# Splitting the float64 weights of a linear-attention and convolution kernel in seven wide tiles instead of fourteen

## The chip, the cores and the metric

The kernel runs on one core of a Trainium2 chip. The time is device microseconds (us) of one execution; a profile of one further execution gives the trace. Line numbers such as L296 are lines of the kernel before the change; the changed kernel has the same statements some 4 to 13 lines further down.

## What is computed

Two stages follow each other. The first is a gated linear attention for 4 batches, 8 heads, 768 time steps and a head size of 48; the second takes its output as x, multiplies by a weight, filters along time, gates and multiplies by a second weight.

```
f = 1 / (1 + exp(-f_logit))
for t in range(768):
    state = f[t][:, None] * state + outer(k[t], v[t])       # 48 x 48 per head
    y[t] = q[t] @ state
x = y with the heads side by side                            # 4 x 768 x 384
h = max(x @ w_in, 0)                                         # 4 x 768 x 1024
conv[t] = conv_w[0]*h[t-1] + conv_w[1]*h[t] + conv_w[2]*h[t+1]
out = (h / (1 + exp(-conv))) @ w_out                         # 4 x 768 x 384
```

`w_in` (384x1024), `conv_w` (3x1024) and `w_out` (1024x384) arrive as float64, two 32-bit words per element.

## The kernel before

**Attention.** Time is cut in 24 chunks of 128 steps (n = 0 to 23, six per batch). For each chunk ScalarE takes two functions of the gate tile `fb` (L376, L378), VectorE scans it (L394), ScalarE makes two exponentials `e` (L397, L399), GpSimd copies their last column to `ft_all` (L401), and VectorE scales keys and queries with them (`kq`, L403). TensorE transposes the keys into `ss` (L409) and forms the scores `A` (L420); VectorE keeps the causal half as `am` (L423). TensorE then sums carried state (L435) and values (L442) into `Y` and makes the new state (L464). ScalarE and VectorE write `Y` as a high and a low part into `xT` (L452, L454), and VectorE updates the state `st` (L471, L474, L476). `Y` and `A` are single PSUM buffers.

**Second stage.** It goes by half batches u = 0 to 7 of three chunks each. When the three chunks of u are in `xT`, six DMAs gather the rows of a fourth slot (L484). For each of 8 blocks f of 128 columns, nine matmuls (L514) form x @ w_in in one of two PSUM buffers `mm`; ScalarE copies it out with a relu into `hb` (L524) and multiplies (L530), VectorE adds two more taps (L534), and for each pair of blocks ScalarE takes a tanh (L538) and VectorE multiplies (L540). A 128-row tile of the output takes a high and a low copy of the gates (L557, L561), 24 matmuls with w_out (L570), a copy to `ob` (L576) and a DMA. All eight blocks of w_out are needed from its first tile on.

**Weights.** Each float64 tile is turned into a float32 sum of two parts, high and low, that TensorE takes in `wi` and `wo`. `split_f64` does it: the raw words come by DMA (`load_raw`, L329); the absolute value of the upper words (ScalarE, L290), a clamp (VectorE, L292), an exclusive or with a shift (L294), a second absolute value (ScalarE, L296), sign and exponent put together (L297), the exponent alone (L299), the high part (ScalarE, L306), and the lower word scaled by the exponent (`ob`, L313). In mode 'd' three matmuls (L318 to L320) then add the pieces in `mm`, and ScalarE or VectorE copies the low part out (L324); in mode 'v' VectorE does it alone (L308, L310, L311). w_in is 6 tiles of 512 columns, w_out 8 tiles of 384; eleven tiles take mode 'd', the last three mode 'v'. The raw words and all intermediate tiles live in buffers that the second stage uses later (`xT`, `g`, `gx`, `ob`).

**Order.** `Plan` decides the order of the instructions on all engines before the program is built: each step has a key from the table `CFG` (a time in chunks plus an offset), an estimated duration in ns, and the buffers that it takes from rings; `Plan.order` plays this through and writes the instructions in the order that it finds. Each engine then works its list strictly in order, and so does SyncE (SP), which issues all DMAs.

Of the kernel before, what the change touches and what calls it, by code (L numbers as in the profile page):

```python
# [174 lines left out]
def gla_moe_kernel(ctx, tc, kq_in, v_in, f_in, w_in, conv_w, w_out, out):  # L175
# [99 lines left out]
    def split_f64(raw, at, r, n, key, need, hi, lo, nm, mode=None):  # L275
        ids = ("raw", raw), ("ms", nm), ("low", nm), ("mm", "pz" + nm)
# [15 lines left out]
        o = step("DVE", 170 + 250 * x, lambda e: V.tensor_scalar(  # L292
            ms(0).bitcast(F32), ms(0).bitcast(F32), F64_LO, F64_HI, ALU.max, ALU.min), [o], use=(1,))
        o = step("DVE", 130 + 385 * x, lambda e: V.tensor_scalar(  # L294
            ms(0), ms(0), 1 << 27, 3, ALU.bitwise_xor, ALU.logical_shift_left), [o], use=(1,))
        o = step("ACT", 160 + 470 * x, lambda e: A.activation(ms(0).bitcast(F32), ms(0).bitcast(F32), AF.Abs), [o], use=(1,))  # L296
        m = step("DVE", 150 + 530 * x, lambda e: V.scalar_tensor_tensor(  # L297
            ms(0), pr(1), -(1 << 31), ms(0), ALU.bitwise_and, ALU.bitwise_or), [o])
        s = step("DVE", 160 + 250 * x, lambda e: V.tensor_scalar(ms(1), ms(0), -(1 << 23), None, ALU.bitwise_and), [m],  # L299
                 use=(1,))  # L300
        mf, sf = (lambda: ms(0).bitcast(F32)), (lambda: ms(1).bitcast(F32))
        if lo is None:
            o = step("DVE", 150 + 530 * x, lambda e: V.scalar_tensor_tensor(
                sf(), pr(0).bitcast(U32), 2.0 ** -52, sf(), ALU.mult, ALU.mult), [s])
            return step("DVE", 150 + 530 * x, lambda e: V.tensor_tensor(hi(), mf(), sf(), ALU.add), [o], use=(1,))
        h = step("ACT", 160 + 460 * x, lambda e: A.copy(hi(), mf()), [m], use=(1,))  # L306
        if mode == "v":
            o = step("DVE", 150 + 530 * x, lambda e: V.scalar_tensor_tensor(  # L308
                sf(), pr(0).bitcast(U32), 2.0 ** -52, sf(), ALU.mult, ALU.mult), [s])
            d = step("DVE", 150 + 530 * x, lambda e: V.tensor_tensor(mf(), mf(), hi().bitcast(F32), ALU.subtract), [h], use=(1,))  # L310
            return step("DVE", 150 + 530 * x, lambda e: V.tensor_tensor(lo(), mf(), sf(), ALU.add), [o, d], use=(1,))  # L311
        low = lambda: plan.buf(ids[2])[:, :n]
        o = step("DVE", 150 + 530 * x, lambda e: V.scalar_tensor_tensor(  # L313
            low(), pr(0).bitcast(U32), 2.0 ** -52, sf(), ALU.mult, ALU.mult), [s], take=(2,))
        pz = lambda: plan.buf(ids[3])[:, :n]

        def join(e):
            nc.tensor.matmul(pz(), ident, mf(), start=True, stop=False)  # L318
            nc.tensor.matmul(pz(), negr, hi(), start=False, stop=False)
            nc.tensor.matmul(pz(), idr, low(), start=False, stop=True)  # L320
# [11 lines left out]
    W_IN, W_OUT = [[None] * KT for _ in range(DFF // WC)], [None] * NF  # L332
    for i in range(DFF // WC):
        for kt in range(KT):
            cs = slice(i * WC, (i + 1) * WC)
            o = load_raw(("wi", i), kt * RW, w_in[kt * P:(kt + 1) * P, cs].bitcast(I32), P, (0.01 * kt, "w1", i), 512, kt == 0)
            W_IN[i][kt] = split_f64(("wi", i), kt * RW, P, WC, (0, "w1s", KT * i + kt), o, lambda kt=kt, cs=cs: wi[:, kt, 0, cs],
                                    lambda kt=kt, cs=cs: wi[:, kt, 1, cs], f"wi{kt}_{i}", CFG["ez"][KT * i + kt])
# [408 lines left out]
```

## Time and profile before

| what | value |
|---|---|
| three timed runs | 339.94 us median (338.13 to 341.12) |
| the profiled execution | 338.65 us, its span 336.9 us, granted TensorE clock 0.994 |
| TensorE matmul (PE) busy | 309.9 us, 92% of the span, 2703 instructions |
| VectorE (DVE) busy | 273.2 us, 81%, 417 instructions |
| ScalarE (ACT) busy | 234.0 us, 69%, 395 instructions |
| GpSimd (POOL) busy | 39.3 us, 12%, 69 instructions |
| chain that ended last | PE 58%, ACT 17%, DMA 13%, DVE 8% |

The span is the time from the first to the last instruction of the profiled execution; 1.75 us of its time lie outside. A busy PE is not yet a PE at its peak: its matmuls are pipelined and a wait shows mainly as the distance between starts. In rows of the time line the first number is the start and the second the duration, both in us; in rows of windows each engine has its busy time and its instruction count.

### The profile page before, as it was taken

Reading aid. Unit: us, or ns where it says so; the run is one execution under the profiler, and the core shown is the slowest. Engines: PE = TensorE matmul, PEld = TensorE weight load, DVE = VectorE, ACT = ScalarE, POOL = GpSimd, SP = SyncE. Lnnn points to the kernel's source line nnn. Section 1 sums busy time; section 2 is a strip of 40 time slices with the busy share of each in tenths; the row PEclk is TensorE's granted clock in tenths of the full one; section 3 lists DMA queues with packets and bytes.
Section 4 is the critical chain, followed back from the end, with each engine's and each line's share of the span. In section 5 each row is a group of like instructions: output and inputs, shape, how many; then the busy total and the mean of one; then the engine's idle time right before and its main releaser. Section 6 shows DMA issues by size and latency. Waiting matters only on the chain.

```text
span 336.9 us, 6805 instructions
## 1 busy us (share of the span) xinstructions
PE 309.9 (92%) x2703; PEld 284.6 (84%) x2703; DVE 273.2 (81%) x417; ACT 234.0 (69%) x395; POOL 39.3 (12%) x69
## 2 busy tenths in 40 slices
PE   0498799989999999999999999999999999999992
PEld 0365478788899899889889999999899999999992
DVE  7989999989999999999999958288768179695210
ACT  6979897689979975799966755464575386684320
POOL 2400100000630006503010210000000001000000
PEclk9999999999999999999999999999999999999997
DMA  7999744620063121655242521121100002101111
GB/s 231 405 402 392 285 136 143 201 106 25 6 211 111 42 70 47 201 161 167 89 137 72 175 60 47 47 74 40 37 0 2 23 26 58 47 2 48 47 46 36
DMA packets 17452, 37.51 MB, mean 111 GB/s; under 512 B 2540, under 2 KB 8708, under 8 KB 17412
## 3 DMA queue, kind: packets, MB, share of 16 engines
q1 hardware_dynamic: 17412, 37.00, 32.6%
q8 instruction: 23, 0.38, 0.5%
q14 instruction: 17, 0.14, 0.1%
HBM read 29.91 MB, written 4.72 MB: 103 GB/s over the span
## 4 chain that ended last, share of the span: by engine, by line
PE 58%; ACT 17%; DMA 13%; DVE 8%; issue 2%; SPq 1%; ACTq 0%; DVEq 0%
PE mm L570 28%; PE mm L514 19%; DMA g<-in_moe_w_out_dram 5%; PE Y L442 4%; ACT g L530 3%; PE A L420 3%; DMA fb<-in_f_logit_dram 3%; DMA xT<-in_moe_w_in_dram 2%; DMA v<-in_v_dram 2%; PE Y L435 2%; ACT hb L524 2%; ACT g L538 1%; DVE am L423 1%; DVE kq L403 1%; ACT fb L376 1%
## 5 line engine op out<-in xcount | busy, mean ns | idle before, releaser
L514 PE MATMUL mm<-xT,wi 128*128 128x384 f32 x576 | 108.1, 341 | 2.3 <-ACT hb L524 1.8
L514 PEld LDWEIGHTS mm<-xT,wi 128*128 128x128 f32 x576 | 99.6, 188 | 4.7 <-ACT hb L524 3.0
L570 PE MATMUL mm<-wo,gx 128*128 128x384 f32 x576 | 103.5, 339 | 0.0
L570 PEld LDWEIGHTS mm<-wo,gx 128*128 128x128 f32 x576 | 101.6, 188 | 0.2 <-issue 0.2
L534 DVE SCALAR_TENSOR_TENSOR g<-hb,cw,g 128x385 f32<-128x385 f32 (+1 forms) x128 | 74.4, 614 | 13.1 <-ACT g L530 11.7
L561 DVE TENSOR_TENSOR gx<-g,gx 128x1024 fp32r<-128x1024 f32 (+2 forms) x28 | 29.8, 1071 | 26.4 <-PE mm L570 23.9
L524 ACT ACTIVATE hb<-mm 128x384 f32<-128x384 f32 x64 | 30.6, 487 | 15.6 <-PE mm L514 15.4
L557 ACT CAST gx<-g 128x1024 fp32r<-128x1024 f32 (+2 forms) x28 | 25.6, 932 | 22.5 <-PE mm L570 18.2
L530 ACT ACTIVATE g<-hb,cw 128x384 f32<-128x384 f32 (+1 forms) x64 | 37.6, 613 | 2.8 <-DVE gx L561 1.7
L420 PE MATMUL A<-kq 48*128 48x128 f32 x384 | 29.7, 297 | 9.7 <-DVE kq L403 8.2
L420 PEld LDWEIGHTS A<-kq 48*128 48x128 f32 x384 | 24.9, 199 | 13.3 <-DVE kq L403 8.5
L538 ACT ACTIVATE g<-g 128x768 f32<-128x768 f32 (+1 forms) x32 | 26.9, 844 | 10.7 <-DVE g L534 10.7
L401 POOL COPY ft_all<-e 128x4 f32<-128x4 f32 x24 | 24.1, 1013 | 86.3 <-ACT e L399 86.0
L540 DVE SCALAR_TENSOR_TENSOR g<-g,hb 128x768 f32<-128x768 f32 (+1 forms) x32 | 30.4, 951 | 3.2 <-ACT g L538 3.0
L423 DVE COPY_PREDICATED am<-mask,A 128x1024 f32<-128x1024 uint8 x24 | 31.6, 1319 | 1.4 <-PE A L420 1.4
L394 DVE TENSOR_TENSOR_SCAN fb<-runs,fb 128x512 f32<-128x512 f32 x24 | 28.8, 1217 | 0.9 <-ACT fb L378 0.7
L403 DVE TENSOR_TENSOR kq<-kq,e 128x1024 f32<-128x1024 f32 x24 | 29.1, 1221 | 0.0
L442 PE MATMUL Y<-am,v 128*48 128x128 f32 (+1 forms) x384 | 26.3, 278 | 0.2 <-DVE am L423 0.2
L442 PEld LDWEIGHTS Y<-am,v 128*48 128x48 f32 (+1 forms) x384 | 20.5, 129 | 4.9 <-issue 3.4
L576 ACT COPY ob<-mm 128x384 f32<-128x384 f32 x24 | 11.4, 475 | 17.8 <-PE mm L570 14.7
L504 POOL COPY hb<-hb 128x4 f32<-128x4 f32 x16 | 12.1, 759 | 88.1 <-DVE g L540 88.0
L452 ACT CAST xT<-Y 112x512 fp32r<-112x512 f32 x24 | 14.0, 582 | 10.2 <-PE Y L464 6.1
(76 smaller groups left out, 291.7 us busy)
## 6 DMA issues: line engine op xcount, KB each, us to landing
kq<-in_kq_dram SPq DMA_DIRECT2D x24, 512.0 KB, 3.9
fb<-in_f_logit_dram SPq DMA_DIRECT2D x24, 256.0 KB, 4.2
v<-in_v_dram SPq DMA_DIRECT2D x24, 192.0 KB, 3.6
out_dram<-ob SPq DMA_DIRECT2D x24, 192.0 KB, 1.9
xT<-in_moe_w_in_dram SPq DMA_DIRECT2D x6, 512.0 KB, 9.5
g<-in_moe_w_out_dram SPq DMA_DIRECT2D x8, 384.0 KB, 6.9
xT<-xT SPq DMA_DIRECT2D x48, 48.0 KB, 2.1
xT<-in_moe_conv_w_dram SPq DMA_DIRECT2D x1, 24.0 KB
```

The lines of the kernel that those rows point to most:

```text
L403: ox = plan.op("DVE", 1222, lambda e, X=X, E=E: nc.vector.tensor_tensor(buf(X), buf(X), buf(E), ALU.mult), ka, need=[o2, ld_x], use=[X, E])
L420: nc.tensor.matmul(buf(("A", n))[:, j, p, :], buf(X)[r, 0, p, :], buf(X)[r, 1, p, :], start=True, stop=True)
L423: o = plan.op("DVE", 1320, lambda e, n=n, AM=AM: nc.vector.copy_predicated(buf(AM), mask, buf(("A", n))), (n, "sc"), need=[o], use=[("A", ...
L442: nc.tensor.matmul(out_of(Y, p, j, w), buf(V).rearrange("p h d -> p (h d)")[:, h * D:h * D + w], buf(AM)[:, j, p, :], start=c == 0 and p < ...
L514: nc.tensor.matmul(buf(ph)[:, :HS], wi[:, t, wl, f * P:(f + 1) * P], x_view(pl, u)[:, t, xl, :], start=(i == 0), stop=(i == 3 * KT - 1))
L524: nc.scalar.activation(hb[:, 2:HS + 2], buf(ph)[:, :HS], AF.Relu, scale=0.5)
L530: o = pl.op("ACT", 620, lambda e, cv=cv, hb=hb, n=n, f=f: nc.scalar.activation(cv(), hb[:, 1:n + 1], AF.Copy, scale=cw[:, 1, f:f + 1]), ke ...
L534: o = pl.op("DVE", 617, lambda e, cv=cv, hb=hb, n=n, f=f, w=w, sh=sh: nc.vector.scalar_tensor_tensor(cv(), hb[:, sh:n + sh], cw[:, w, f:f ...
L538: o = pl.op("ACT", 846, lambda e, cv=cv: nc.scalar.activation(cv(), cv(), AF.Tanh), key, need=last, use=[("g", u)], mode="T")
L540: gates[u, fp] = pl.op("DVE", 960, lambda e, cv=cv, fp=fp, n=n: nc.vector.scalar_tensor_tensor(cv(), cv(), 1.0, h_b[:, fp:fp + 2, 1:n + 1] ...
L561: los.append(pl.op("DVE", 150 + 134 * nn * NF // 128, lambda e, hv=hv, lv=lv, src=src: nc.vector.tensor_tensor(lv(), src(), hv().bitcast(F ...
L570: nc.tensor.matmul(buf(po)[:, :DM], view(g)[:, f, :], wo[:, f, wl, :], start=(i == 0), stop=(i == 3 * NF - 1))
```

## The change

Two neighbouring weight tiles go through `split_f64` together: w_in as 3 tiles of 1024 columns (rows 0 and 1 of the left half, the whole of row block 2, rows 0 and 1 of the right half), w_out as 4 tiles of 768. The matmuls of mode 'd' still work on halves of 512 or 384, since `mm` holds no more, and each half has its own copy out. Mode 'v' is left for the last pair only. The exclusive or and the second absolute value become one mask with the shift. The exponent goes to a buffer of its own from a new ring `mt`. All offsets of `CFG` are new. The core of the diff:

```diff
-CFG = dict(..., w1=(2.8, 3.89), w1s=(5.26, -3.21, -10.27, -9.05, -4.36, -8.77), cw=-15.73, w2=(7.75, 23.68), ...,
-           ez='dddddddddddvvv')
+CFG = dict(..., w1=(1.34, 5.48, 6.21), w1s=(-2.97, -1.48, 2.66), cw=-19.2, w2=(10.83, 20.68), ...,
+           ez='ddddddv')
...
-            pl.ring("ms", [(new("gx", [P, RW], I32, 4), [("gx", i)]) for i in (0, 2)])
-            pl.ring("low", [(new("ob", [P, WC], F32R, 2), [("ob", i)]) for i in range(2)])
+            pl.ring("ms", [(new("gx", [P, RW], I32, 4), [("gx", i)]) for i in (0, 1)])
+            pl.ring("mt", [(new("gx", [P, RW], I32, 4), [("gx", i)]) for i in (2, 3)])
+            pl.ring("low", [(new("ob", [P, RW], F32R, 2), [("ob", i)]) for i in range(2)])
...
-        o = step("DVE", 130 + 385 * x, lambda e: V.tensor_scalar(
-            ms(0), ms(0), 1 << 27, 3, ALU.bitwise_xor, ALU.logical_shift_left), [o], use=(1,))
-        o = step("ACT", 160 + 470 * x, lambda e: A.activation(ms(0).bitcast(F32), ms(0).bitcast(F32), AF.Abs), [o], use=(1,))
-        m = step("DVE", 150 + 530 * x, lambda e: V.scalar_tensor_tensor(
-            ms(0), pr(1), -(1 << 31), ms(0), ALU.bitwise_and, ALU.bitwise_or), [o])
+        o = step("DVE", 155 + 265 * x, lambda e: V.tensor_scalar(
+            ms(), ms(), (1 << 27) - 1, 3, ALU.bitwise_and, ALU.logical_shift_left), [o], use=(1,))
+        m = step("DVE", 150 + 540 * x, lambda e: V.scalar_tensor_tensor(
+            ms(), pr(1), -(1 << 30), ms(), ALU.bitwise_and, ALU.bitwise_or), [o])
...
+        for z in range(2):
+            pz = ("pz", nm, z)
+            def join(e, z=z, pz=pz):
+                to, w = plan.buf(pz)[:, :n // 2], slice(z * n // 2, (z + 1) * n // 2)
+                nc.tensor.matmul(to, ident, mf()[:, w], start=True, stop=False)
+                nc.tensor.matmul(to, negr, hi()[:, z], start=False, stop=False)
+                nc.tensor.matmul(to, idr, low()[:, w], start=False, stop=True)
...
+    for i, g in enumerate((0, 2, 1)):
+        for z in range(2):
+            kt, c0 = (2, z * WC) if g == 2 else (z, g * WC)
```

Three places show how the order changes. The first is VectorE at the start of the program, from the scans of the first gate tiles (`fb`) to the first scores; `gx` is the working tile of a weight split. Before:

```order
L394 SCALAR_TENSOR_TENSOR fb_105<-runs,fb_105 128x512 x2
L345 COPY cw<-mm_119 128x24
L394 SCALAR_TENSOR_TENSOR fb_105<-runs,fb_105 128x512
L394 SCALAR_TENSOR_TENSOR fb_106<-runs,fb_106 128x512 x2
L403 TENSOR_TENSOR kq_107<-kq_107,e_115 128x1024
L403 TENSOR_TENSOR kq_108<-kq_108,e_116 128x1024
L394 SCALAR_TENSOR_TENSOR fb_106<-runs,fb_106 128x512
L423 COPY_PREDICATED am_86<-mask_84,A 128x1024
L292 TENSOR_SCALAR gx_206<-gx_206 128x512
L403 TENSOR_TENSOR kq_109<-kq_109,e_115 128x1024
L294 TENSOR_SCALAR gx_206<-gx_206 128x512
```

The same place on VectorE with the change:

```order
L407 SCALAR_TENSOR_TENSOR fb_105<-runs,fb_105 128x512
L357 COPY cw<-mm_119 128x24
L407 SCALAR_TENSOR_TENSOR fb_105<-runs,fb_105 128x512 x2
L407 SCALAR_TENSOR_TENSOR fb_106<-runs,fb_106 128x512 x3
L295 TENSOR_SCALAR gx_178<-gx_178 128x1024
L416 TENSOR_TENSOR kq_107<-kq_107,e_115 128x1024
L296 TENSOR_SCALAR gx_178<-gx_178 128x1024
L416 TENSOR_TENSOR kq_108<-kq_108,e_116 128x1024
L298 SCALAR_TENSOR_TENSOR gx_178<-xT_138,gx_178 128x1024
L436 COPY_PREDICATED am_86<-mask_84,A 128x1024
L300 TENSOR_SCALAR gx_221<-gx_178 128x1024
```

The sixth scan and the clamp of the first weight tile now stand ahead of the first key scaling, and the first weight tile is worked between the first chunks.

The second place is TensorE around the first matmuls of the second stage (x @ w_in of u = 0). Before:

```order
L420 MATMUL A<-kq_108 128x128 x8
L318 MATMUL mm_119<-gx_412,ident 128x384
L319 MATMUL mm_119<-wo,negr 128x384
L320 MATMUL mm_119<-ob_502,idr 128x384
L409 MATMUL ss_101<-ident,kq_108 128x128 x4
L514 MATMUL mm_120<-xT_295,wi 128x384 x9
L435 MATMUL Y<-kq_107,st_90 48x128
```

With the change TensorE has there:

```order
L433 MATMUL A<-kq_108 128x128 x8
L422 MATMUL ss_101<-ident,kq_108 128x128 x4
L527 MATMUL mm_119<-xT_293,wi 128x384 x9
L527 MATMUL mm_120<-xT_293,wi 128x384 x9
L323 MATMUL mm_119<-gx_372,ident 128x512
L324 MATMUL mm_119<-wi,negr 128x512
L325 MATMUL mm_119<-ob_497,idr 128x512
L323 MATMUL mm_120<-gx_372,ident 128x512
L324 MATMUL mm_120<-wi,negr 128x512
L325 MATMUL mm_120<-ob_497,idr 128x512
```

Ahead of the first block there are two of the 384-wide joins in place of one, and four of the 512-wide in place of five; the blocks and the joins of one tile now come in pairs.

The third place is TensorE around the first matmuls with w_out (L570, with the change L583). Before:

```order
L420 MATMUL A<-kq_109 128x128 x8
L409 MATMUL ss_101<-ident,kq_109 128x128 x4
L570 MATMUL mm_119<-wo,gx_980 128x384 x16
L570 MATMUL mm_119<-wo,gx_1004 128x384 x8
L570 MATMUL mm_120<-wo,gx_1032 128x384 x16
L570 MATMUL mm_120<-wo,gx_1102 128x384 x8
L514 MATMUL mm_119<-xT_726,wi 128x384 x9
```

With the change the same engine has:

```order
L527 MATMUL mm_120<-xT_473,wi 128x384 x9
L583 MATMUL mm_119<-wo,gx_789 128x384 x16
L583 MATMUL mm_119<-wo,gx_803 128x384 x8
L583 MATMUL mm_120<-wo,gx_874 128x384 x16
L583 MATMUL mm_120<-wo,gx_897 128x384 x8
L433 MATMUL A<-kq_110 128x128 x8
L583 MATMUL mm_119<-wo,gx_912 128x384 x16
L583 MATMUL mm_119<-wo,gx_935 128x384 x8
L422 MATMUL ss_101<-ident,kq_110 128x128 x4
```

Here `A` of chunk 10 (the `kq_109` shown before is that of n = 10) stood ahead of these matmuls; with the change they come after all blocks of u = 1, and `A` of chunk 7 comes behind the second output tile. The attention runs some three chunks later against the second stage.

More of the change, by code (lines that the diff above doesn't have):

```diff
@@ L280, in pr, with tmp, parts @@
             return plan.buf(ids[0])[:r, at:at + 2 * n].rearrange("p (n w) -> p n w", w=2)[:, :, w]
-        def ms(i):
-            return plan.buf(ids[1])[:r, i * WC:i * WC + n]
+        def tmp(i):
+            return plan.buf(ids[i])[:r, :n]
+        def parts(ap, like):
+            return ap.rearrange("p (a n) -> p a n", a=2) if len(like.shape) == 3 else ap
         def step(eng, ns, run, need, use=(0, 1), take=()):
             return plan.op(eng, ns, lambda e: run(e), key, need=need, use=[ids[i] for i in use],
-                           take=[(("raw", "ms", "low", "mm")[i], ids[i]) for i in take])
+                           take=[(("raw", "ms", "mt", "low")[i], ids[i]) for i in take])
@@ new lines, in split_f64 @@
+        o = step("ACT", 160 + 465 * x, lambda e: A.activation(mf(), pr(1).bitcast(F32), AF.Abs), need, use=(0,), take=(1,))
+        o = step("DVE", 155 + 265 * x, lambda e: V.tensor_scalar(mf(), mf(), F64_LO, F64_HI, ALU.max, ALU.min), [o], use=(1,))
+        o = step("DVE", 155 + 265 * x, lambda e: V.tensor_scalar(
+            ms(), ms(), (1 << 27) - 1, 3, ALU.bitwise_and, ALU.logical_shift_left), [o], use=(1,))
+        m = step("DVE", 150 + 540 * x, lambda e: V.scalar_tensor_tensor(
+            ms(), pr(1), -(1 << 30), ms(), ALU.bitwise_and, ALU.bitwise_or), [o])
@@ L302, in split_f64 @@
+        s = step("DVE", 155 + 265 * x, lambda e: V.tensor_scalar(st(), ms(), -(1 << 23), None, ALU.bitwise_and), [m],
+                 use=(1,), take=(2,))
         if lo is None:
[L303 to L306, printed above, removed]
+            o = step("DVE", 150 + 540 * x, lambda e: V.scalar_tensor_tensor(
+                sf(), pr(0).bitcast(U32), 2.0 ** -52, sf(), ALU.mult, ALU.mult), [s], use=(0, 2))
+            return step("DVE", 150 + 540 * x, lambda e: V.tensor_tensor(hi(), mf(), sf(), ALU.add), [o], use=(1, 2))
@@ L307, in split_f64 @@
+        h = step("ACT", 160 + 455 * x, lambda e: A.copy(hi(), parts(mf(), hi())), [m], use=(1,))
         if mode == "v":
[L308 to L320, printed above, removed]
@@ L322, in split_f64 @@
-        o = plan.op("PE", 60 + 1350 * x, join, key, need=[h, o], use=[ids[1], ids[2]], take=[("mm", ids[3])], mode="r")
-        return plan.op(dict(ACT=140 + 480 * x, DVE=150 + 530 * x), 0,
-                       lambda e: (A.copy if e == "ACT" else V.tensor_copy)(lo(), pz()), key, need=[o], use=[ids[3]])
+            o = step("DVE", 150 + 540 * x, lambda e: V.scalar_tensor_tensor(
+                sf(), pr(0).bitcast(U32), 2.0 ** -52, sf(), ALU.mult, ALU.mult), [s], use=(0, 2))
+            d = step("DVE", 150 + 540 * x, lambda e: V.tensor_tensor(
+                parts(mf(), hi()), parts(mf(), hi()), hi().bitcast(F32), ALU.subtract), [h], use=(1,))
@@ new lines, in split_f64 @@
+            return [step("DVE", 150 + 540 * x, lambda e: V.tensor_tensor(
+                lo(), parts(mf(), lo()), parts(sf(), lo()), ALU.add), [o, d], use=(1, 2))]
+        low = lambda: plan.buf(ids[3])[:, :n]
+        o = step("DVE", 150 + 540 * x, lambda e: V.scalar_tensor_tensor(
+            low(), pr(0).bitcast(U32), 2.0 ** -52, sf(), ALU.mult, ALU.mult), [s], use=(0, 2), take=(3,))
+        done = []
+        for z in range(2):
[5 more added lines that the diff above has]
+                nc.tensor.matmul(to, idr, low()[:, w], start=False, stop=True)
+            j = plan.op("PE", 60 + 675 * x, join, key, need=[h, o], use=[ids[1], ids[3]], take=[("mm", pz)], mode="r")
+            done.append(plan.op(dict(ACT=140 + 240 * x, DVE=150 + 265 * x), 0, lambda e, z=z, pz=pz: (
+                A.copy if e == "ACT" else V.tensor_copy)(lo()[:, z], plan.buf(pz)[:, :n // 2]), key, need=[j], use=[pz]))
@@ L326, in load_raw @@
+        return done
     def load_raw(raw, at, src, r, key, nbytes, take):
@@ L330, in load_raw @@
                        take=[("raw", i)] if take else [], use=[] if take else [i], size=nbytes)
[L332 to L338, printed above, removed]
+    W_IN, W_OUT = [[] for _ in range(2)], []
+    for i, g in enumerate((0, 2, 1)):
+        o = []
+        for z in range(2):
+            kt, c0 = (2, z * WC) if g == 2 else (z, g * WC)
+            o.append(load_raw(("wi", i), z * RW, w_in[kt * P:(kt + 1) * P, c0:c0 + WC].bitcast(I32), P,
+                              (0.01 * z, "w1", i), 512, z == 0))
+        part = lambda z, g=g: (wi[:, 2, z, :].rearrange("p (a n) -> p a n", a=2) if g == 2 else
+                               wi[:, 0:2, z, g * WC:(g + 1) * WC])
+        o = split_f64(("wi", i), 0, P, 2 * WC, (0, "w1s", i), o, lambda part=part: part(0), lambda part=part: part(1),
+                      f"wi{i}", CFG["ez"][i])
+        for k in ((0, 1) if g == 2 else (g,)):
+            W_IN[k] += o
     nk = conv_w.shape[0]
```

34 lines of the change are left out of this document (14 added, 20 removed).

## Prediction

> **What bounds the kernel now.** I read the windows first, to see which engine is full in which stage, then the time line around each wait of TensorE, and last the chain that ended last. In the windows the columns are the stretch, then for each engine its busy us and its instruction count, the granted clock, the DMA share and GB/s.
>
> ```profile
> 8.00:16.00 8.00, 2.64 (x19) 2.42 (x20) 7.98 (x9) 7.75 (x15) 3.49 (x4) 1.00 1.02 404
> 40.00:48.00 8.00, 7.31 (x99) 5.57 (x95) 8.00 (x17) 7.21 (x11) 0.13 (x1) 1.00 0.51 141
> 120.00:330.00 210.00, 209.14 (x1724) 199.86 (x1723) 158.63 (x218) 132.43 (x217) 21.38 (x33) 1.00 0.21 67
> ```
>
> In both stretches before 48 us VectorE (the third engine) is full; from 120 us on TensorE has 209.14 of 210 us. The chain closes with TensorE alone:
>
> ```profile
> 288.48 12.72 PE mm L514 x72
> 301.20 29.69 PE mm L570 x168
> ```
>
> So a block of nine L514 takes 1.59 us (12.72/8), 24 L570 take 4.24, and the end is the sum of TensorE's work plus the gaps in it. All weight splitting lies in the first 105 us. The change can help only by closing gaps there, and anything it adds to TensorE shows in full.
>
> The gaps, from starts on TensorE:
>
> ```profile
> 13.36 2.08 PE L420 MATMUL A<-kq 48*128 48x128 f32 x16 [7.52 <-DVE kq L403]
> 45.64 1.16 PE L420 MATMUL A<-kq 48*128 48x128 f32 x16 [0.69 <-DVE kq L403]
> 48.20 1.81 PE L514 MATMUL mm<-xT,wi 128*128 128x384 f32 x9
> 73.02 6.51 PE L514 MATMUL mm<-xT,wi 128*128 128x384 f32 x36 [1.06 <-ACT hb L524]
> 86.52 1.84 PE L514 MATMUL mm<-xT,wi 128*128 128x384 f32 x9 [0.45 <-ACT hb L524]
> 112.00 3.72 PE L514 MATMUL mm<-xT,wi 128*128 128x384 f32 x18 [0.36 <-ACT ob L576]
> ```
>
> Up to the first block at 48.20 the waits are for VectorE. After it TensorE runs on without a wait until 71 us, and the later ones are ScalarE's and short.
>
> **The change, first term: VectorE until the first block.** VectorE's prices are distances between starts, since it runs gapless here:
>
> ```profile
> 8.62 3.44 DVE L394 TENSOR_TENSOR_SCAN fb<-runs,fb 128x512 f32<-128x512 f32 x3
> 12.08 2.36 DVE L403 TENSOR_TENSOR kq<-kq,e 128x1024 f32<-128x1024 f32 x2
> ...
> 29.68 0.42 DVE L292 TENSOR_SCALAR gx<-gx 128x512 f32<-128x512 f32 x1
> 30.02 0.42 DVE L299 TENSOR_SCALAR gx<-gx 128x512 int32<-128x512 int32 x1
> 30.35 0.42 DVE L294 TENSOR_SCALAR gx<-gx 128x512 int32<-128x512 int32 x1
> 30.69 0.69 DVE L313 SCALAR_TENSOR_TENSOR ob<-xT,gx 128x512 fp32r<-128x512 uint32 x1
> 31.29 1.22 DVE L403 TENSOR_TENSOR kq<-kq,e 128x1024 f32<-128x1024 f32 x1
> 32.43 0.68 DVE L297 SCALAR_TENSOR_TENSOR gx<-xT,gx 128x512 int32<-128x512 int32 x1
> ...
> 41.01 0.36 DVE L474 TENSOR_TENSOR st<-Y,st 112x192 f32<-112x192 f32 x1
> 41.28 0.36 DVE L294 TENSOR_SCALAR gx<-gx 128x384 int32<-128x384 int32 x1
> 41.55 0.36 DVE L476 TENSOR_TENSOR st<-st,ft_all 112x192 f32<-112x192 f32 x1
> 41.81 0.70 DVE L454 TENSOR_TENSOR xT<-Y,xT 112x512 fp32r<-112x512 f32 x1
> 42.41 0.56 DVE L297 SCALAR_TENSOR_TENSOR gx<-g,gx 128x384 int32<-128x384 int32 x1
> 42.88 1.34 DVE L423 COPY_PREDICATED am<-mask,A 128x1024 f32<-128x1024 uint8 x1
> 44.08 0.38 DVE L299 TENSOR_SCALAR gx<-gx 128x384 int32<-128x384 int32 x1
> ```
>
> A scan costs 1.15 us ((12.08-8.62)/3). An operation with one source costs 0.335 at 512 columns and 0.27 at 384; with two sources 0.60 at 512, 0.47 at 384, and 1.14 at 1024 (31.29 to 32.43). A state step costs 0.27, an xT 0.60, an am 1.20. The wide one-source forms do not occur in this trace. By the slope from 384 to 512 they cost 0.60 at 1024 and 0.47 at 768, which is my value; the bounds are two narrow ones (0.67) and the price of two sources at that width (1.14). Two sources at 768 lie midway between 512 and 1024, 0.87. A pair of 512 tiles then costs 2x(3x0.335+2x0.60)=4.41 narrow and 3x0.60+2x1.14=4.08 wide, 0.33 less; a pair of 384 tiles 3.50 against 3.15.
>
> Now count what VectorE does from its first scan to the third L454, chunk 2's, behind which u = 0 is gathered. Keys, scores and states are the same in number. Before: 8 scans, one low-part copy (L324 at 512, taken at 0.60), five whole 512 tiles, and L292 and L294 of a 384 tile. After: 7 scans, two whole 1024 tiles, one whole 768 tile. The difference is -1.15 -0.60 -5x2.205 -2x0.27 +2x4.08 +3.15 = **-2.0 us**. Only 0.5 of that is real saving; the rest is work put behind this point, and TensorE has by then done 0.3 us less (below). With VectorE's waits unchanged the third L454 starts at 39.8 instead of 41.81, and the first block at 46.2 instead of 48.20.
>
> On the way the start gets worse: the first kq now follows six scans and a wide clamp instead of five scans, so `A` of chunk 0 starts 1.75 us later. VectorE has work meanwhile, so it costs nothing beyond the sum above. SP issues the first two weight loads ahead of all four kq: 1.05 MB at 404 GB/s, 2.6 us. The first kq was in by 12.08 at the latest, so by 14.7; it is wanted at 13.8. The bounds are 0 and 0.9 us; I take 0, the end it is nearer to: in the rows above the first kq starts where the scans end (8.62+3.44), so the load was not what it waited for.
>
> **Second term: TensorE's joins.** From 52.00 to 53.10 and from 65.48 to 66.89 one join passes:
>
> ```profile
> 52.00 0.91 PE L318 MATMUL mm<-gx,ident 128*128 128x384 f32 x2
> 53.10 1.73 PE L514 MATMUL mm<-xT,wi 128*128 128x384 f32 x9
> 65.48 1.02 PE L318 MATMUL mm<-gx,ident 128*128 128x512 f32 x2
> 66.89 1.16 PE L420 MATMUL A<-kq 48*128 48x128 f32 x16
> ```
>
> That is 1.10 at 384 and 1.41 at 512. Before there are six of 512 and five of 384; after, six and six, since one tile changes from 'v' to 'd': **+1.1 us**. Ahead of the first block stand four and two in place of five and one, so **+0.3** moves behind it. Nothing hides either.
>
> **Third term: ScalarE.** All fourteen second absolute values go:
>
> ```profile
> L296 ACT ACTIVATE gx<-gx 128x384 f32<-128x384 f32 x8 | 4.2, 527 | 1.6 <-DVE gx L294 1.6
> L296 ACT ACTIVATE gx<-gx 128x512 f32<-128x512 f32 x6 | 3.8, 625 | 1.2 <-DVE gx L294 1.1
> ```
>
> That is 8.0 us of ScalarE and two queue hops per tile, against three more copies out of `mm`, which I price like L296 at the same width (VectorE made two of eleven, now ScalarE makes all twelve), and two more table loads in the new order. Little of it stood on the path before 48 us. After it, ScalarE's lateness made the three gaps above, 1.87 us. A block still needs the same copies, and the wide L290 and L306 hold ScalarE about a us at a time, so I let **-1.0** of the 1.87 go, with bounds of 0 and -1.87.
>
> **Fourth term: VectorE against TensorE from the first block to chunk 7.** After the change all sixteen blocks of u = 0 and 1 and two output tiles stand on TensorE ahead of `A` of chunk 7, whose kq is far down VectorE's list. TensorE's prices:
>
> ```profile
> 138.11 1.09 PE A L420 x16
> 139.20 0.59 PE ss L409 x4
> 139.79 0.59 PE Y L435 x11
> ...
> 141.40 1.02 PE Y L442 x16
> ...
> 147.42 0.48 PE Y L464 x13
> ```
>
> TensorE: 16x1.59 + two output tiles 8.48 + joins 2x1.41+4x1.10 + `A` 1.09 + ss 0.59 + carries 1.18 + values 3.06 + states 0.96 = 48.0, so it reaches that `A` at 46.2+48.0 = 94.2. VectorE: 32 taps at 0.53, 7 gate products and 4 steps of the last weight pair at 0.87, 3 low parts and 2 kq at 1.14, 3 am at 1.20, one scan, 4 xT at 0.60, 5 states at 0.27, the rest of one 1024 and two 768 tiles (0.47 or 0.60 for one source) = 53, from 40.4 (the third L454's end) to 93.4, and kq itself ends at 94.6. They tie. From 12.08 to 41.81 VectorE had 5 kq, 3 scans, 4 am, 2 xT, 5 states and the weight work above, 28.7 us of the 29.7, so it waited about 1 us; at that rate I charge **+0.1 to +0.5**, say +0.3, with 3 us as upper bound.
>
> ```profile
> 74.31 4.86 DVE L534 SCALAR_TENSOR_TENSOR g<-hb,cw,g 128x384 f32<-128x384 f32 x9 [1.12 <-ACT g L530]
> ```
>
> (That row gives 0.53 to 0.54 for a tap.) Behind chunk 7 the order is spread more evenly, and TensorE has far more work than VectorE (209 against 159 us in the last long window); I take its few gaps there as unchanged.
>
> **Sum.** -2.0 +0.3 +1.1 -1.0 +0.3 = **-1.3 us**. The profiled execution had 338.65 us (span 336.9), so 337.35. The median of the timed runs, 339.94, lies 1.3 above that execution; on its scale the forecast is **338.6 us**. One per cent, 3.4 us, is about what a measurement of this kernel can tell from no change, and the forecast is inside it.
>
> **Rivals.** *The gaps close almost wholly.* With less fixed work on both engines VectorE's 1 us of waits before the first block goes, ScalarE's three gaps vanish (0.9 more), the tie costs nothing (0.3) and so do the gaps after 120 us (210-209.14, 0.9): 3.1 better, 335.5. For it speaks that ScalarE loses most of 8 us; against it that ScalarE was not what VectorE waited for most.
>
> *VectorE comes last at chunk 7.* This is the slower side. Everything that VectorE waits between 40 and 94 us beyond the tie goes one to one to TensorE, whose list is fixed; the forecast's 1.3 us are gone at 1.3 us of waits beyond the 0.3, and from there on the kernel is slower than before. Taps wait for ScalarE's L530 (1.12 in the row above) and ScalarE's wide steps stand ahead of some of them. At 3 us more it gives 341.6, at 5 us 343.6. Against it: before the change VectorE waited only about 1 us in 30.
>
> *The wide forms do not do what they say.* If one-source work at 1024 and 768 ran at the two-source price, 9 such operations of 1024 would cost 0.54 more each and 12 of 768 0.40, together 9.7 us on VectorE, all of it before chunk 7, where VectorE ties or comes last: 348.3. The 384 and 512 rows, where one source costs half, speak against it.
>
> *GpSimd's copy is held out.* One ft_all copy took 5.59 us and the next 0.18:
>
> ```profile
> 88.46 5.59 POOL L401 COPY ft_all<-e 128x4 f32<-128x4 f32 x1 [0.74 <-ACT e L399]
> 95.46 0.18 POOL L401 COPY ft_all<-e 128x4 f32<-128x4 f32 x1
> ```
>
> VectorE was gapless beside the long one. If wide steps held the copy longer, the state update that reads it would wait at the head of VectorE's list, but then VectorE idles and the copy needs 0.18; over the eight chunks until 105 us that is 1.4 us at most, or 340.0. [...]
>
> **How the numbers follow.** Forecast, 336.5 to 340.5: 0.48. Gaps close, 333 to 336.5: 0.28. VectorE last at chunk 7: 0.14, of it a third beyond 343.3. Wide forms slow: 0.04. GpSimd: 0.06. Faster by over 1% (below 336.5) comes from the second case and a little of the first: 0.30. Slower by over 1% (above 343.3): 0.10. Within 1%: 0.60. The range of 8 in 10 is 334.5 to 342.5.
>
> **What would show it.** One-source steps of 0.68 us duration at 1024 (0.60 from start to start), the first `A` near 15.1, the first block near 46.2, six 512 and six 384 joins, no second absolute value, `A` of chunk 7 waiting under 1 us for VectorE near 95, and TensorE's last matmul near 329.6 instead of 330.9 (301.20+29.69). The prediction is wrong if the first block comes later than 48, if TensorE waits for a gather (L484) of u = 2 with the attention three chunks later, or if a gap of several us opens after 120 us.

## The result, and the profile after

The changed kernel takes **336.72 us** (median of 22 runs, 334.76 to 339.67); the kernel before, on the same chip, 339.15 (22 runs, 338.13 to 341.43). The ratio is 0.9929, 95% interval 0.9905 to 0.9954: a gain of 2.4 us, 0.7%, inside the bound of one per cent that the prediction named. The profiled execution took 336.67 us (span 334.9) against 338.65 (336.9) before, so 1.98 less. Ratios leave out the seven executions that took over 1.5% longer than the fastest of their kernel on that chip; the profiled one of the run called e4 below was among them (396.93 us at a granted clock of 0.758), so its rows are not read.

The windows of the changed kernel, in the three stretches that the prediction quoted for before, and from 48 to 105 us:

```profile
8.00:16.00 8.00, 0.64 (x6) 0.64 (x8) 8.00 (x9) 7.26 (x14) 1.21 (x2) 1.00 1.02 398
40.00:48.00 8.00, 7.18 (x85) 5.64 (x84) 8.00 (x13) 5.57 (x9) 0.00 (x0) 1.00 0.48 138
48.00:105.00 57.00, 56.65 (x453) 50.90 (x452) 57.00 (x82) 45.39 (x75) 9.91 (x11) 1.00 0.27 85
120.00:330.00 210.00, 208.08 (x1800) 197.56 (x1798) 156.07 (x221) 133.93 (x216) 13.19 (x30) 1.00 0.24 72
```

VectorE (the third engine) is full in the first three. From 40 to 48 us ScalarE (the fourth) has 5.57 us instead of 7.21; only 0.52 of that is a second absolute value, the rest is work that the new order puts elsewhere. From 48 to 105 us both TensorE (56.65 of 57 us, before 55.41) and VectorE (57.00, before 55.69) are full. The 208.08 us in the last row are less than before mainly because the last matmul now ends at 329.03.

TensorE's time line of the changed kernel, by start and duration, at the places the forecast rested on:

```profile
15.36 2.08 PE L433 MATMUL A<-kq 48*128 48x128 f32 x16 [9.86 <-DVE kq L416]
45.42 1.16 PE L433 MATMUL A<-kq 48*128 48x128 f32 x16 [0.63 <-DVE kq L416]
46.93 3.37 PE L527 MATMUL mm<-xT,wi 128*128 128x384 f32 x18
73.87 13.47 PE L527 MATMUL mm<-xT,wi 128*128 128x384 f32 x72
87.19 8.64 PE L583 MATMUL mm<-wo,gx 128*128 128x384 f32 x48
95.76 1.16 PE L433 MATMUL A<-kq 48*128 48x128 f32 x16
```

The first block of the second stage starts at 46.93 instead of 48.20. The three waits at 73.02, 86.52 and 112.00 have no counterpart: 72 matmuls of u = 1 run through from 73.87, and w_out follows without a wait. One wait for ScalarE is left further on, 0.55 at 138.54, where before had 0.34 at 164.86. The end of the chain is again TensorE alone:

```profile
300.40 3.18 PE mm L527 x18
303.58 25.45 PE mm L583 x144
```

So the last matmul ends at 329.03 instead of 330.89. I split the difference at the first block. It starts 1.27 us earlier. From there to the last matmul's end there were 282.69 us (330.89-48.20), and now 282.10, although 1.4 us of joins were expected to come into this stretch.

### The profile page after: what moved, and what is told of

Read it like the earlier page. It is cut to its first block, busy times and chain, and to the rows that moved or that the text cites. A ratio compares the mean times of both kernels' runs of the same rounds, so it can differ in the third digit from the quotient of the medians.

```text
span 334.9 us, 6741 instructions
## 1 busy us (share of the span) xinstructions
PE 311.0 (93%) x2707; PEld 287.0 (86%) x2707; DVE 269.8 (81%) x380; ACT 229.6 (69%) x367; POOL 31.0 (9%) x69
## 4 chain that ended last, share of the span: by engine, by line
PE 63%; DVE 19%; ACT 10%; issue 3%; DMA 3%; SPq 1%; DVEq 0%; ACTq 0%
PE mm L583 31%; PE mm L527 18%; DVE g L547 4%; PE A L433 4%; PE Y L455 4%; DMA fb<-in_f_logit_dram 3%; PE Y L448 2%; DVE am L436 2%; DVE kq L416 2%; DVE fb L407 2%; PE ss L422 2%; DVE xT L467 1%; DVE gx L298 1%; PE Y L477 1%; DVE g L553 1%
## 5 line engine op out<-in xcount | busy, mean ns | idle before, releaser
L583 PE MATMUL mm<-wo,gx 128*128 128x384 f32 x576 | 104.3, 340 | 0.1
L583 PEld LDWEIGHTS mm<-wo,gx 128*128 128x128 f32 x576 | 101.5, 188 | 0.8 <-ACT hb L537 0.4
L543 ACT ACTIVATE g<-hb,cw 128x384 f32<-128x384 f32 (+1 forms) x64 | 38.4, 616 | 2.3 <-DVE gx L574 1.1
L570 ACT CAST gx<-g 128x1024 fp32r<-128x1024 f32 (+2 forms) x28 | 25.9, 934 | 19.4 <-PE mm L583 15.9
L433 PEld LDWEIGHTS A<-kq 48*128 48x128 f32 x384 | 24.9, 199 | 15.2 <-DVE kq L416 10.9
L414 POOL COPY ft_all<-e 128x4 f32<-128x4 f32 x24 | 17.0, 709 | 88.4 <-ACT e L412 88.4
L517 POOL COPY hb<-hb 128x4 f32<-128x4 f32 x16 | 11.0, 685 | 105.7 <-DVE g L553 105.7
```

Source lines behind the costliest of these rows:

```text
L433: nc.tensor.matmul(buf(("A", n))[:, j, p, :], buf(X)[r, 0, p, :], buf(X)[r, 1, p, :], start=True, stop=True)
L543: o = pl.op("ACT", 620, lambda e, cv=cv, hb=hb, n=n, f=f: nc.scalar.activation(cv(), hb[:, 1:n + 1], AF.Copy, scale=cw[:, 1, f:f + 1]), ke ...
L583: nc.tensor.matmul(buf(po)[:, :DM], view(g)[:, f, :], wo[:, f, wl, :], start=(i == 0), stop=(i == 3 * NF - 1))
```

## The experiments

All were timed against the kernel before on the chip they ran on, and each ratio is to those runs. First block, last matmul and the time between come from the one profiled execution of each. Executions differ at the start: the changed kernel's first block came at 46.93 and, in e10, at 46.67.

| kernel | median, us | ratio to before, 95% | first block | last matmul ends | between |
|---|---|---|---|---|---|
| before | 339.15 | 1 | 48.20 | 330.89 | 282.69 |
| changed | 336.72 | 0.9929 [0.9905, 0.9954] | 46.93 | 329.03 | 282.10 |
| e1 half-width steps | 338.47 | 0.9974 [0.9947, 1.0002] | 47.02 | 330.99 | 283.97 |
| e2 second absolute value back | 340.0 | 1.0014 [0.9989, 1.004] | 46.67 | 332.19 | 285.52 |
| e3 48 spare matmuls | 338.37 | 0.9949 [0.9915, 0.9983] | 47.01 | 328.54 | 281.53 |
| e4 wide tiles, old offsets | 341.05 | 1.0041 [1.0012, 1.0071] | not read | not read | not read |
| e5 34 spare matmuls | 335.4 | 0.9892 [0.9852, 0.9932] | 45.89 | 327.40 | 281.51 |
| e6 two pairs in mode 'v' | 341.65 | 1.0061 [1.0035, 1.0087] | 47.52 | 335.66 | 288.14 |
| e7 mask alone, in before | 338.44 | 0.9981 [0.995, 1.0013] | 50.64 | 332.36 | 281.72 |
| e8 27 spare matmuls in before | 337.75 | 0.9956 [0.9926, 0.9986] | 49.10 | 331.37 | 282.27 |
| e9 spare matmuls, also in gaps | 334.62 | 0.9869 [0.9818, 0.992] | 44.98 | 326.64 | 281.66 |
| e10 changed kernel, beside e9 | 336.17 | 0.9892 [0.9849, 0.9934] | 46.67 | 329.01 | 282.34 |

**e1: the width alone.** The order of the changed kernel stays, but each wide step is issued as two instructions of half the width:

```diff
-        m = step("DVE", 150 + 540 * x, lambda e: V.scalar_tensor_tensor(
-            ms(), pr(1), -(1 << 30), ms(), ALU.bitwise_and, ALU.bitwise_or), [o])
+        m = step("DVE", 150 + 540 * x, each(lambda e, z, c: V.scalar_tensor_tensor(
+            ms()[:, c], pr(1)[:, c], -(1 << 30), ms()[:, c], ALU.bitwise_and, ALU.bitwise_or)), [o])
```

> The changed kernel in the same order, with each wide step of the seven splits (five on VectorE, two on ScalarE) issued as two instructions of half the width; matmuls as they are. Theory A (the gain is the fixed part of an instruction that wide tiles save): VectorE gets 2.3 us back (0.33 per pair of tiles), ScalarE some 1.8, the first block comes near 47.4 instead of 46.9, and the ratio to the kernel before goes from 0.993 to 0.996 or more. Theory B (the gain is the new order, the width is of no account): the ratio stays at 0.993, first block at 46.9 to 47.1.

By the medians some two thirds of the gain went (0.9974), though the two intervals just touch. The first block came only 0.09 later, but its start is no price of the width: here VectorE waited 0.62 us for the first xT, in the changed kernel 1.95 (below). The rest was lost behind the first block. The xT of the last chunk of u = 1 and the gather that it releases, first on VectorE and SP of the changed kernel:

```profile
68.56 0.69 DVE L467 TENSOR_TENSOR xT<-Y,xT 112x512 fp32r<-112x512 f32 x1
69.28 4.00 SPq L497 DMA_DIRECT2D xT<-xT  x6
```

and the same steps with half-width steps, with what TensorE then waited for:

```profile
69.49 0.70 DVE L474 TENSOR_TENSOR xT<-Y,xT 112x512 fp32r<-112x512 f32 x1
70.22 4.00 SPq L504 DMA_DIRECT2D xT<-xT  x6
75.90 3.92 PE L534 MATMUL mm<-xT,wi 128*128 128x384 f32 x21 [0.16 <-DMA xT<-xT]
80.27 8.55 PE L534 MATMUL mm<-xT,wi 128*128 128x384 f32 x45 [0.45 <-ACT hb L544]
88.66 8.63 PE L590 MATMUL mm<-wo,gx 128*128 128x384 f32 x48
```

VectorE is 0.93 us later at that xT, the gather goes out 0.94 later, TensorE waits for it and then for ScalarE, and w_out starts at 88.66 instead of 87.19. So the time that wide steps save is needed where this order has no slack.

**e2: the second absolute value alone.** Same order, with the activation put back behind the mask:

```diff
+        def mask(e):
+            V.tensor_scalar(ms(), ms(), (1 << 27) - 1, 3, ALU.bitwise_and, ALU.logical_shift_left)
+            if lo is not None:
+                A.activation(mf(), mf(), AF.Abs)
```

> The changed kernel in the same order, with a second absolute value put back on ScalarE in each of the seven splits, between the mask and the step that joins sign and exponent (it changes no value). Theory C (the gain comes from the absolute value that was left out): ScalarE gets some 6.5 us back (0.83 and 1.05 us each) and VectorE waits for it in each chain; the waits of TensorE for ScalarE between the first block and 115 us come back, 1.5 to 2 us, ratio 0.997 to 1.000. Theory B: ScalarE has room, ratio 0.993 to 0.995.

The whole gain is gone, more than the 0.997 to 1.000 expected, and the trace shows most of it. ScalarE and TensorE around the third w_in tile's joins:

```profile
44.01 1.06 ACT L299 ACTIVATE gx<-gx 128x1024 f32<-128x1024 f32 x1 [2.01 <-DVE gx L297]
53.55 0.84 ACT L299 ACTIVATE gx<-gx 128x768 f32<-128x768 f32 x1 [0.56 <-DVE gx L297]
54.30 1.06 ACT L332 CAST wi<-mm 128x512 fp32r<-128x512 f32 x2
51.37 1.13 PE L327 MATMUL mm<-gx,ident 128*128 128x512 f32 x2 [1.32 <-ACT hb L541]
54.92 3.39 PE L531 MATMUL mm<-xT,wi 128*128 128x384 f32 x18 [0.65 <-ACT wi L332]
```

The absolute value of this tile waits 2.01 us for VectorE at the head of ScalarE's list; the first copy of a block (`hb`) then starts at 50.79 instead of 49.50, and the joins wait 1.32 for it. The absolute value of the next tile waits 0.56, the low-part copies L332 stand behind it, and TensorE's next blocks start at 54.92; in the changed kernel they start at 52.80. A third wait for ScalarE, 1.60 at 141.67 where the changed kernel has 0.55, lies behind all weights, and why it grew is open. So the step that the edit took away cost ScalarE's time (0.84 and 1.06 us) and was a place where its list waited for VectorE; no run separates the two.

**e4: the order alone.** The tiles stay wide, and every offset that is not the weights' own gets its old value:

```diff
-            a=17.29, ft=-1.2, b=0.21, sc=-0.63, va=0.44, st=-5.04, ga=-14.63, ...
+            a=19.28, ft=-1.2, b=-0.52, sc=-0.75, va=0.15, st=-2.21, ga=-17.4, ...
```

> The changed kernel with the offsets of everything but the weight steps as they were before; only those of the weight loads and splits, which count other tiles, stay new. Theory B (the gain is the new order): the gain is lost, ratio 0.998 or more. Theory A or C (width, or the absolute value): 0.991 to 0.995.

It is slower than before by 0.4%: wide tiles in an order not chosen for them are no gain. The mix of old and new offsets is a third order, not that of before, so this is no price of the order alone.

**e7: the mask alone, in the kernel before.** Its own order and narrow tiles; nothing is issued in place of the second absolute value:

```diff
-            ms(0), ms(0), 1 << 27, 3, ALU.bitwise_xor, ALU.logical_shift_left), [o], use=(1,))
-        o = step("ACT", 160 + 470 * x, lambda e: A.activation(ms(0).bitcast(F32), ms(0).bitcast(F32), AF.Abs), [o], use=(1,))
+            ms(0), ms(0), (1 << 27) - 1, 3, ALU.bitwise_and, ALU.logical_shift_left), [o], use=(1,))
+        o = step("ACT", 160 + 470 * x, lambda e: None, [o], use=(1,))
```

> The kernel before in its own order and with its 14 narrow tiles; only the exclusive or and the second absolute value become the one mask, so 14 ACT operations (8.0 us of ScalarE) and their two hops are gone, and nothing is moved. Theory of the third term: ScalarE's lateness made the gaps of 1.06, 0.45 and 0.36 us at 71 to 112 us; 1.0 of the 1.87 closes and the tiles before 48 us come a little sooner: 1 to 2 us less, ratio 0.994 to 0.997. Rival (each part only counts in an order made for it): the order of before waits for other things at the same places, ratio 0.998 to 1.002.

By the time it is undecided (0.9981, with 1 inside the interval). Its TensorE rows show two opposite effects:

```profile
20.58 2.08 PE L420 MATMUL A<-kq 48*128 48x128 f32 x16 [0.35 <-DVE am L423]
50.64 1.81 PE L514 MATMUL mm<-xT,wi 128*128 128x384 f32 x9
75.29 6.53 PE L514 MATMUL mm<-xT,wi 128*128 128x384 f32 x36 [0.88 <-ACT hb L524]
```

Behind the first block 0.97 us went (282.69 to 281.72): of the three waits for ScalarE the first fell from 1.06 to 0.88 and the other two are gone. But the first block came 2.44 later, in an execution where TensorE's third `A` still took 2.08 us; in the profile of before that `A`, at 20.74, took 1.16.

**e6: fewer joins.** `ez='dddddvv'`, planned anew:

> The changed kernel with the last two weight pairs in mode 'v' in place of one (same offsets, planned anew, order alike up to about 62 us). Theory of the second term: a pair of joins is 2.2 us of TensorE that nothing hides, so the time falls by up to 2.2 against the changed kernel, ratio to the kernel before about 0.986, for 1.8 us more on VectorE. Rival: the order is what the gain hangs on; the plan moves the attention of chunks 7 and 10 ahead of blocks of u = 1 again, gaps open behind 70 us, and the ratio is 0.995 or above.

The rival held. The plan moved the attention again, and TensorE waited for gathers, ScalarE and VectorE; the longest of its waits:

```profile
74.14 0.79 PE L527 MATMUL mm<-xT,wi 128*128 128x384 f32 x3 [0.67 <-DMA xT<-xT]
80.32 1.83 PE L527 MATMUL mm<-xT,wi 128*128 128x384 f32 x9 [0.86 <-ACT hb L537]
114.65 18.75 PE L583 MATMUL mm<-wo,gx 128*128 128x384 f32 x96 [2.67 <-ACT gx L570]
```

2.1 us less of joins brought 6.6 us more at the last matmul (335.66 against 329.03) in this execution, the longest of its twelve (343.67; the median is 341.65). It says nothing on a join's price, only on the order's.

**e3, e5, e8, e9, e10: the start.** VectorE waited 1.95 us in the changed kernel where the forecast had it busy. Its row, and ScalarE's list ahead of the xT that it waits for:

```profile
28.84 0.36 DVE L484 TENSOR_TENSOR st<-Y,ft_all 112x192 f32<-112x192 f32 x1 [1.95 <-ACT xT L465]
41.14 0.69 DVE L467 TENSOR_TENSOR xT<-Y,xT 112x512 fp32r<-112x512 f32 x1
25.17 0.59 ACT L328 CAST wi<-mm 128x512 fp32r<-128x512 f32 x1 [2.85 <-PE mm L325]
26.63 0.59 ACT L328 CAST wi<-mm 128x512 fp32r<-128x512 f32 x1 [0.87 <-PE mm L325]
27.11 0.63 ACT L410 ACTIVATE e<-fb 128x512 f32<-128x512 f32 x1
27.64 0.62 ACT L389 ACTIVATE fb<-fb 128x512 f32<-128x512 f32 x1
28.16 0.57 ACT L465 CAST xT<-Y 112x512 fp32r<-112x512 f32 x1
```

ScalarE waits for two joins, and xT stands behind their copies. TensorE ran both `A` ahead of them (2.08 instead of 1.16 us) and the first of these joins (its first two matmuls 1.91 instead of 1.02) at half rate; the second, from 24.93, was nearly at full rate (1.19 for the same two). So spare matmuls, whose sums nobody reads, were put on TensorE behind its first transpose, in the same order (e5 has 34, e3 48, e8 27 in the kernel before):

```diff
+        for _ in range(34):
+            nc.tensor.matmul(ps_s[1][:, :P], ident, ident, start=True, stop=True)
```

> The changed kernel in the same order, with 48 spare matmuls of 128x128 on TensorE behind the transpose of conv_w, from 5 us to about 14.5 us, into a bank that nothing uses then. Theory D (the start fell short of the forecast since TensorE's first matmuls run at half rate and VectorE's first state step at 28.8 us waits for them): scores at 1.09 us instead of 2.08 from the first one on, the 1.95 us wait of VectorE ahead of that state step shrinks to under 0.7, the first block near 45.7 instead of 46.9, ratio 0.989 to 0.990. Rival (that wait is for ScalarE or for the load of v, whatever TensorE does): first block stays at 46.5 to 46.9, ratio 0.993.

> The changed kernel, same order, with 34 spare 128x128 matmuls (sum thrown away) on TensorE after its first transpose, so that it is busy from 5.4 to about 14.9 us (48 of them took 12.9 us in e3 and held the first A to 18.2). Theory: VectorE's 1.95 us wait at 28.8 is the cold TensorE (A 2.08 instead of 1.16 us) through ScalarE's list: the two low-part copies L328 wait for joins that end late, and xT L465 stands three activations behind them. Then A runs in 1.16 from 15.4 on, the wait for xT falls under 0.7, the third xT (L467) comes near 39.8 instead of 41.1, the first block near 45.6 instead of 46.9, and the time falls by about 1.3 against the changed kernel: ratio to the kernel before about 0.989. Rival: other waits take its place, as in e3 (e L410 for kq), or TensorE loses the gain again behind the first block: first block within 0.3 of 46.9 and ratio 0.992 to 0.995.

> The kernel before in its own order, with 27 spare 128x128 matmuls on TensorE from 5.8 to about 13.2 us, ahead of the first A. Theory: cold matmuls cost this kernel too (A 2.08 us at 13.36 and 17.27; VectorE waits 0.80 and 0.82 for them): first block (L519 here) near 47 instead of 48.2 and ratio about 0.996. Rival: what VectorE waits for in this order is ScalarE's second absolute values, not TensorE; first block within 0.3 of 48.2, ratio 0.999 to 1.001.

In e3 the spare matmuls ran until 18.2 us and held `A` up by 3 us; the wait for xT fell to 0.68, but VectorE waited 1.63 for `A`, the first block was no earlier, and that run does not decide. In e5 they ended at 15.8, and the first block came at 45.89, 1.04 earlier, for a ratio of 0.9892. But the wait for xT only fell to 1.54, and TensorE, whose first `A` had taken 1.16 us, went back to half rate. TensorE's rows of e5, then its windows with the granted clock as third number from the end:

```profile
18.86 1.16 PE L438 MATMUL A<-kq 48*128 48x128 f32 x16 [0.90 <-DVE am L441]
20.66 0.72 PE L427 MATMUL ss<-ident,kq 128*128 128x128 f32 x4 [0.63 <-DVE kq L421]
21.17 1.92 PE L323 MATMUL mm<-gx,ident 128*128 128x512 f32 x2
```

```profile
18.00:20.00 2.00, 1.14 (x16) 0.97 (x16) 2.00 (x3) 2.00 (x4) 0.00 (x0) 1.00 1.03 408
20.00:22.00 2.00, 1.37 (x7) 0.88 (x6) 2.00 (x3) 1.75 (x3) 0.20 (x1) 0.77 1.01 382
22.00:24.00 2.00, 2.00 (x5) 1.26 (x4) 2.00 (x4) 0.03 (x1) 0.30 (x1) 0.50 1.06 384
```

e8 gave the time expected (0.9956), but its profiled execution, at 338.95 one of its longer ones, does not show the step: first block at 49.10 and a half-rate join at 21.19 there too (1.93 us for its first two matmuls). So e9 has 33 spare matmuls ahead, 4 before the second `A` and 3 behind it, in the gaps of 0.90 and 0.63:

> The changed kernel, same order, with 33 spare matmuls ahead of the first A, 4 more ahead of the second A and 3 behind it, where TensorE waited 0.90 and 0.63 us in e5 and then ran its next five joins' matmuls at half rate (1.92 and 1.41 us at a granted clock of 0.50 to 0.77). Theory: it now stays at full rate, the joins end near 24.3 instead of 25.6, the two low-part copies and the first xT on ScalarE come up to 0.9 earlier (then bound by the key at 25.1 and two activations), VectorE's wait for xT falls from 1.54 to about 0.6, the first block comes near 45.0 and the ratio to the kernel before is 0.986. Rival: that wait is ScalarE's own list (two activations ahead of xT) and not the clock: wait still above 1.3, first block 45.7 to 46, ratio 0.989.

> The changed kernel itself, beside e9 on one chip. If the spare matmuls bring what e5 showed, it is 1 to 2.5 us above e9; ratio to the kernel before as at first, 0.990 to 0.995. Rival: e5's 0.989 was this kernel's own spread, and both come out alike.

e9's TensorE row of the first join, VectorE's wait, the third xT, and TensorE's first block:

```profile
21.09 1.02 PE L324 MATMUL mm<-gx,ident 128*128 128x512 f32 x2
26.92 0.36 DVE L494 TENSOR_TENSOR st<-Y,ft_all 112x192 f32<-112x192 f32 x1 [0.68 <-ACT xT L475]
39.21 0.68 DVE L477 TENSOR_TENSOR xT<-Y,xT 112x512 fp32r<-112x512 f32 x1
44.98 3.40 PE L537 MATMUL mm<-xT,wi 128*128 128x384 f32 x18
```

The joins are at full rate (1.02 us for the first two matmuls), the wait is 0.68 instead of 1.95, the first block comes at 44.98, and the median of 334.62 is the best of all. But not all of this is the spare matmuls' doing. VectorE's second scan, first in the changed kernel, then in e9, and ScalarE's row ahead of it in the changed kernel:

```profile
7.90 5.68 DVE L407 TENSOR_TENSOR_SCAN fb<-runs,fb 128x512 f32<-128x512 f32 x5 [1.26 <-ACT fb L391]
6.83 5.78 DVE L413 TENSOR_TENSOR_SCAN fb<-runs,fb 128x512 f32<-128x512 f32 x5 [0.21 <-ACT fb L397]
6.72 0.63 ACT L389 ACTIVATE fb<-fb 128x512 f32<-128x512 f32 x1 [0.94 <-DMA fb<-in_f_logit_dram]
```

ScalarE waited 0.94 us for the DMA of a gate tile, issued by 4.05 us, ahead of TensorE's first matmul at 5.23; in e9 it did not wait. So these scans began 1.07 earlier in e9 by the chance of one execution (7.57 in e10, 7.32 in e5). Counted from this scan, the first block takes 39.03 us in the changed kernel, 39.10 in e10, 38.57 in e5 and 38.15 in e9: some 0.5 us is the gain of e5 and 0.9 that of e9, not 1.04 and 1.95.

Nor are spare matmuls the only way to full rate. In e6, which has none and has the same order up to there, the first join and VectorE's wait were

```profile
21.38 1.02 PE L323 MATMUL mm<-gx,ident 128*128 128x512 f32 x2
27.84 0.36 DVE L484 TENSOR_TENSOR st<-Y,ft_all 112x192 f32<-112x192 f32 x1 [0.69 <-ACT xT L465]
```

The half rate came later in that execution (joins of 2.08 at 32.09). Taken together, the wait for xT was 0.68 in e3, 0.69 in e6 and 0.68 in e9, where both joins ran at full rate (1.02 us for the first two matmuls of each), and 1.95, 1.31 and 1.54 in the changed kernel, e10 and e5, where the first ran at half rate (1.91, 1.91 and 1.92). (In e2 the first ran at half rate too, 1.91, and the wait was 0.84, but there VectorE had already waited 0.86 for the absolute value put back.) So these executions show the longer wait with the half rate; that the seven matmuls in the gaps kept it away in e9 rests on one execution.

On time, the rival of e10 is not out for e5: e10, without any spare matmul, has the same ratio of 0.9892. For e9 the medians lie 1.55 apart on one chip, and five of its six runs are below all six of e10, but the two ratios' intervals overlap. So the spare matmuls' worth is shown as to the place, and its size in time only roughly.

## Why the prediction was right

The forecast was 338.6 us with a range of 334.5 to 342.5; the time is 336.72, 1.9 below the forecast. On its own scale, profile against profile, it said -1.3 and got -1.98. Some 0.8 of the 1.9 is the scale: the median of three runs lay 1.3 above the profiled execution, that of 22 runs 0.5. Step by step:

**First term, prices: right.** Wide one-source steps were to take 0.68 us, 0.60 from start to start at 1024 columns, and 0.47 at 768. VectorE's rows of the changed kernel:

```profile
13.51 0.67 DVE L295 TENSOR_SCALAR gx<-gx 128x1024 f32<-128x1024 f32 x1
14.09 1.22 DVE L416 TENSOR_TENSOR kq<-kq,e 128x1024 f32<-128x1024 f32 x1
15.22 0.68 DVE L296 TENSOR_SCALAR gx<-gx 128x1024 int32<-128x1024 int32 x1
15.83 1.22 DVE L416 TENSOR_TENSOR kq<-kq,e 128x1024 f32<-128x1024 f32 x1
```

That is 0.58 and 0.61 to the next start; at 768 columns it was 0.46 (34.91 to 35.37). The rival of slow wide forms is out.

**First term, size: too large.** The sum gave the third xT at 39.8 "with VectorE's waits unchanged"; it came at 41.14. The waits were not unchanged. The wait of 0.80 for `A` went, but a wait of 1.95 for xT came, and the second scan began 0.49 later (7.90 against 7.41) with the landing of a gate tile, which is chance: 7.57 in e10. That is 1.64 too late, and 0.3 less work than the sum had. The step that failed is "VectorE has work meanwhile, so it costs nothing", said of the later first `A`. VectorE had work, but TensorE's first join ran at half rate (1.91 us for its first two matmuls; before the change 1.12), ScalarE's list waited for it, and VectorE stood for an xT at the end of that list; where the joins ran at full rate that wait was 0.7. The late `A` alone does not make the joins slow: in e6 it came at 14.85 and they were not (1.02). The prediction's own rows showed `A` at 2.08 and at 1.16 us, and it gave the difference no price. From xT to the first block it then took 5.79 instead of the 6.4 carried over from before, since no 384 join (1.11, 46.73 to 47.84) stands behind the last `A`. The term measured -1.27 instead of -2.0, and -1.76 counted from the second scan.

**Second term: right.** Six 512 and six 384 joins passed; a pair took 2.66 us at 512 (50.14 to 52.80) and 2.08 at 384 (61.37 to 63.45), so 1.33 and 1.04 each instead of 1.41 and 1.10.

**Third term: too small.** The forecast let 1.0 of the 1.87 us of waits for ScalarE go. All three are gone, and from the first block to the end some 2.0 us closed (1.4 of joins expected, 0.59 us less in all); of this the waits in TensorE's rows account for 1.7 (2.73 before, 1.00 after). e7 closes 0.97 in the old order with the mask alone, what the forecast had taken; in the new order taking the mask away costs about the whole gain (e2). How much belongs to the order none of these runs shows.

**Fourth term: 0 instead of +0.3.** The tie was there: the key of chunk 7 stands on VectorE in

```profile
94.14 1.22 DVE L416 TENSOR_TENSOR kq<-kq,e 128x1024 f32<-128x1024 f32 x1
95.27 0.96 DVE L553 SCALAR_TENSOR_TENSOR g<-g,hb 128x770 f32<-128x770 f32 x1
```

It was done by 95.3, and TensorE reached that `A` at 95.76 and did not wait: half a microsecond of slack. VectorE had no idle time from 48 to 105 us, so the charge for its waits was not needed; its 53 us of work from the third xT to that key measured 52.4 (41.75 to 94.14).

**Rivals.** ScalarE's three gaps closed wholly, as the first rival had it, but the VectorE waits at the start did not go. VectorE was not last at chunk 7, and TensorE did not wait for a gather. GpSimd's copy did not hold VectorE up: the waits name ScalarE's xT, and the copies became shorter, not longer:

```profile
L414 POOL COPY ft_all<-e 128x4 f32<-128x4 f32 x24 | 17.0, 709 | 88.4 <-ACT e L412 88.4
```

The mean is 709 ns, where before it was 1013; the rival's 1.4 us did not occur. What made one copy take 5.59 us before is not shown: at 95.46, where the next took 0.18, VectorE was busy without a gap too.

So the sum came out close partly by luck, since misses of opposite sign met: 0.7 too much at the start, 1.0 and 0.3 too little behind it.

## What to carry to other kernels

When an edit comes with a new order, width, removed steps and order are not separate gains: half-width steps cost about two thirds of the gain (e1), the second absolute value all of it (e2), and a mixed order more than all (e4). A step that is late on one in-order engine is priced by what stands behind it on every list it touches, not by whether one engine has other work meanwhile. Where the first matmuls come late and scattered, spare matmuls that end just as the first real one is ready are worth a trial: in e5, counted from the second scan, the first block came some 0.5 us earlier; in e3, where they ended 3 us too late, the first block came no earlier. Before one execution's start is read as an effect, look where its first loads landed: here that alone moved the start by up to 1.07 us.
